# Transposing four units of q and k by DMA instead of TensorE in a fused sparse attention and MLP kernel

## The chip, the core and the metric

The kernel runs on one core of a Trainium2 chip. Five engines run their own instruction streams in order and wait for one another through semaphores: TensorE (PE; its weight loads are shown as PEld), VectorE (DVE), ScalarE (ACT), GpSimd (POOL) and SyncE (SP). SP and POOL issue nearly all DMAs here, each through its own queue; sixteen DMA engines serve both queues. The metric is the device time of one execution in microseconds (us), as the median of several runs.

## The reference

```
q, k, v: (8 batches, 8 heads, 576 tokens, 64), float32
scores = q k^T / 8
heads 0-3 (local):   key j allowed for query i when 0 <= i - j < 32
heads 4-7 (strided): key j allowed when j <= i and j % 32 == i % 32
x = softmax(scores) v, heads side by side: (4608 tokens, 512)
out = relu(x w_in)^2 w_out        w_in: 512 x 2048, w_out: 2048 x 512
```

## The kernel before

Attention of a later batch is woven into the dense work of an earlier one. The dense work runs in nine chunks of 512 tokens. Each chunk has 16 groups of `mm1` (four matmuls of 128x512 each; ACT applies relu, line 713, and DVE squares, line 714) and then 16 groups of `mm2` (four matmuls each; after every fourth, ACT copies the result and SP stores it, lines 733 and 737). `mm1` of chunk 1 writes to two PSUM banks in turn (the pool "ph"). Groups are numbered through: 0 to 15 are `mm1` of chunk 0, 16 to 31 its `mm2`, 32 to 47 `mm1` of chunk 1, 48 to 63 its `mm2`, and so on.

The order of everything else is written out by hand in the string PLAN. A line "35: T8kv" says that step T of unit 8, name k, with its copy on DVE ("v"; "a" is ACT), is put into the instruction streams just before group 35. No scheduler changes this order, so an instruction that waits holds everything behind it on its engine.

A unit u is a batch and a pair of heads: batch u // 4, pair u % 4. Units 8 and 9 are the local heads of batch 2, units 12 and 13 those of batch 3. The local scores (step S, line 505) need q and k with the 64 channels of two heads on the partitions and the tokens in order along the free axis. For batches up to 3 this takes these steps:

- `l` (lines 281 to 292): POOL issues a DMA that loads q or k of both units, float32 to bf16, into a part of `xt` that is not in use yet. Each of 96 partitions gets six neighbouring tokens, so rows are long.
- `c` (cast_qk_local, line 297): a copy on DVE or ACT rearranges one unit into a tile of `qk_in`.
- `T` (step_T, lines 448 to 461): six TensorE transposes (line 453) into a PSUM bank, then one copy (line 460) from PSUM that also brings the tokens into order: on the partition axis they came as "p", in the six blocks as "j", and the copy writes "(p j)".

The results lie in `qT` (a ring of four buffers) and `kTl` (four buffers, chosen by `v_slot`). Local heads of batches 4 to 7 load rows in another shape (step Q, line 278) and are transposed by DMA straight into place (step Y, transpose_local, line 378).

The strided heads of a batch take: C (line 349), a POOL load of q or k rows into `q_t` or `k_t`, one buffer each; X (line 354), a transposing DMA on SP into `qT_s` or `kT_s`; k (lines 365, 368), copies of k into block-diagonal form `kb`; s (line 574), scores, an exponential on ACT and a mask on DVE; x (lines 585 and 588), sums and outputs, a logarithm and an exponential on ACT (590, 591) and products on DVE (598, 604) into `xt`. Since `q_t` and `k_t` have one buffer each, C of the next batch waits on POOL until X of this one has landed. A step "s2.0" is part 0 for batch 2.

Other steps named below: D (line 667) is the product of local weights and v; E brings its result into `xt`, from batch 2 on by a transposing DMA on SP (line 682 in the profile); V and U load v; B copies v into block-diagonal form (line 397).

SP's queue holds, in program order, the transposing DMAs (X, Y, E) and the output stores.

Of the kernel before, what the change touches and what calls it, by code (L numbers as in the profile page):

```python
# [9 lines left out]
BF16 = mybir.dt.bfloat16  # L10
# [18 lines left out]
6: o2 l2k8+9 mv0g o3 mk0g  # L29
10: c4qv  # L30
11: c4kv
12: l2q8+9 T4qa
13: c5qv c5ka T4kv
14: W1q0v T5qa
15: S4!
16: W1q1v T5ka
# [5 lines left out]
22: B11v l3k12+13 s1.2 U2  # L42
23: E4a D5.1
24: x1.0
26: X2k l3q12+13 x1.1
28: V3 E5a x1.2
29: c9kv
30: c8qv
31: c8ka c9qv X2q
34: C3q  # L50
35: T8kv
37: T9kv
38: T8qv C3k
41: S8!
42: T9qa
44: S9! D8.0 k20v
45: D8.1 k21v
46: B20v
47: E8 D9.0 B21v U3
48: Q16k s2.0  # L60
49: D9.1
50: Q17q Q16q c12kv s2.1
51: c12qa E9 s2.2
52: Q17k c13kv c13qa
54: x2.0
55: X3q X3k
56: x2.1 C4k C4q
57: T12ka
58: V4 T13qv T12qa
59: T13ka  # L70
60: x2.2 B30v
61: B31v
63: U4 S12!
# [83 lines left out]
def kernel(  # L157
# [9 lines left out]
    nc = tc.nc  # L167
    B, H, S, D = q.shape
    d_model, d_ff = moe_w_in.shape
    T = B * S  # L170
# [3 lines left out]
    QL = 96  # L174
# [15 lines left out]
    qkT = ctx.enter_context(tc.tile_pool(name="qkT", bufs=4))  # L190
# [17 lines left out]
    def bank(nm):  # L208
        if places:
            return all_banks[places.pop(0)]  # L210
        t = banks[nm].pop(0)
        banks[nm].append(t)
        while id(t) in unread:
            run_due(lambda x: x[1] == unread[id(t)])
        return t
# [10 lines left out]
    NV = 4  # L226
# [12 lines left out]
    kTl = [singles.tile([128, 32 + S], BF16, name=f"kTl{i}") for i in range(NV)]  # L239
# [18 lines left out]
    units = [(b, p) for b in range(B) for p in range(H // 2)]  # L258
    st = {}
# [34 lines left out]
    def cast_qk_local(u, name, copy):  # L294
        s = st[u]
        t = qk_in.tile([QL, 6, 2, D], BF16, name=f"{name}_l")
        copy(t.rearrange("p j h d -> p h j d"), s[name + "f"].rearrange("p h (j d) -> p h j d", j=6))
        s[name] = t
# [16 lines left out]
    def step_TS(b, name, g, copy):  # L315
        src = str_rows[b, name]
        pt = bank("pt").bitcast(BF16)[:, 0:S]
        if b:
            for i in range(NJ):
                c = 128 * (NJ * g + i)  # L320
                nc.tensor.transpose(pt[:, SP_ * i:SP_ * (i + 1)], src[:, c:c + 128], ident[0:SP_, 0:SP_])
            if g == 0:
                o = strTs[name].tile([128, NP2 * SR], BF16, name=f"{name}T_s")
                str_T[b, name] = o.rearrange("c (a p) -> c a p", p=SR)
            copy(str_T[b, name][:, NJ * g:NJ * (g + 1), 0:SP_], pt.rearrange("c (a p) -> c a p", p=SP_))
            return
        for i in range(2):
            for s3 in range(NP3):
                c = 128 * (2 * g + i)
                o = S // 2 * i + QL * s3  # L330
                nc.tensor.transpose(pt[:, o:o + QL], src[:, s3, c:c + 128], ident[0:QL, 0:QL])
        if g == 0:
            o = strTs[name].tile([128, 2 * NJ * SR], BF16, name=f"{name}T_s")
            str_T[b, name] = o[:, 0:2 * NJ * SP_].rearrange("c (a r) -> c a r", a=NJ // 2)
        o = str_T[b, name]
        copy(o[:, 2 * g:2 * g + 2, :].rearrange("c a r -> c (a r)"), pt)
        if g == 1:
            for i in range(2):
                st.setdefault(2 + i, {})[name + "T"] = \
                    o[:, :, 2 * SP_ * i:2 * SP_ * (i + 1)].rearrange("c a (h p) -> c h a p", h=2)  # L340
# [11 lines left out]
    def transpose_str(b, name):  # L352
        o = strTs[name].tile([128, NP2 * SR], BF16, name=f"{name}T_s").rearrange("c (a p) -> c a p", p=SR)
        nc.sync.dma_start_transpose(out=o, in_=big.pop((b, name)))
        str_T[b, name] = o
# [14 lines left out]
    def transpose_local(u):  # L370
        s = st[u]
        for name in "qk":
            if name == "k":
                full = kTl[v_slot(u)]
                dst = full[:, 32:32 + S]
            else:
                full = dst = qkT.tile([128, S], BF16, name="qT")
            nc.sync.dma_start_transpose(out=dst.rearrange("c (t p) -> c t p", p=QL),
                                        in_=s[name].rearrange("p t h d -> p (t h d)"))
            s[name + "T"] = full  # L380

    def v_slot(u):
        b, p = units[u]
        return (b * 2 + p % 2) % NV
# [23 lines left out]
    def shift_v_local(b, copy):  # L408
        t = vl_all[:, (2 * b) % NV:(2 * b) % NV + 2].rearrange("p u h t d -> p (u h) t d")
        copy(t[0:32, :, 1:NL, 0:D], t[96:128, :, 0:NL - 1, 0:D])  # L410
# [37 lines left out]
    def step_T(u, name, copy):  # L448
        s = st[u]
        src = s[name].rearrange("p j h d -> p (j h d)")  # L450
        pt = bank("pt").bitcast(BF16)[:, 0:S]
        for j in range(6):
            nc.tensor.transpose(pt[:, QL * j:QL * (j + 1)], src[:, 128 * j:128 * (j + 1)],  # L453
                                ident[0:QL, 0:QL])
        if name == "k":
            full = kTl[v_slot(u)]
            dst = full[:, 32:32 + S]
        else:
            full = dst = qkT.tile([128, S], BF16, name="qT")
        copy(dst.rearrange("c (p j) -> c p j", j=6), pt.rearrange("c (j p) -> c p j", j=6))  # L460
        s[name + "T"] = full
# [278 lines left out]
    A, V, G = nc.scalar.copy, nc.vector.tensor_copy, nc.gpsimd.tensor_copy  # L740
    ENG = {"a": A, "v": V, "g": G}
# [18 lines left out]
    def warm(n):  # L760
        if n:
            pw = bank("py")
            for _ in range(n):
                nc.tensor.matmul(pw, idle[:, 0:128], idle, start=True, stop=True)
# [3 lines left out]
    def first_part(kks, ffs):  # L768
        for ff in ffs:
            mm1(0, ff, kks, FIRST, None if ff < 2 else "py")  # L770

    def run_step(word):
        word, _, at = word.partition("/")
        places[:] = [int(x) for x in at.split(",") if x]
        op, arg = word[0], word[1:]
        if op == "w":
            warm(int(arg))
        elif op == "c":
            cast_qk_local(int(arg[:-2]), arg[-2], ENG[arg[-1]])
        elif op == "T":  # L780
            step_T(int(arg[:-2]), arg[-2], ENG[arg[-1]])
        elif op == "W":
            step_TS(int(arg[0]), arg[1], int(arg[2]), ENG[arg[3]])
        elif op == "S":
            u, _, half = arg.rstrip("!").partition(".")
            step_S(int(u), int("!" in arg), [int(half)] if half else range(2))
        elif op == "G":
            step_G(int(arg))
        elif op == "b":
            step_B(*(int(x) for x in arg.split(".")))  # L790
        elif op == "N":
            step_N(int(arg))
        elif op == "O":
            step_O(int(arg))
        elif op in "sx":
            (step_SS if op == "s" else step_XX)(*(int(x) for x in arg.split(".")))
        elif op == "k":
            step_K(int(arg[0]), int(arg[1]), ENG[arg[2]])
        elif op == "m":
            memset_later(arg[:-1], nc.gpsimd if arg[-1] == "g" else nc.vector)  # L800
        elif op == "D":
            if "." in arg:
                u, part = arg.split(".")
                step_D(int(u), int(part))
            else:
                step_D0(int(arg))
        elif op == "E":
            step_E(int(arg.rstrip("av")), ENG.get(arg[-1]))
        elif op == "P":
            first_part(*([int(x) for x in y] for y in arg.split(".")))  # L810
        elif op == "H":
            shift_v_local(int(arg[:-1]), ENG[arg[-1]])
        elif op == "C":
            load_str_tall(int(arg[:-1]), arg[-1])
        elif op == "Q":
            load_qk_rows(int(arg[:-1]), arg[-1])
        elif op == "X":
            transpose_str(int(arg[:-1]), arg[-1])
        elif op == "Y":
            transpose_local(int(arg))  # L820
        elif op == "V":
            load_v_local_all(int(arg))
        elif op == "U":
            load_v_str(int(arg))
        elif op == "B":
            spread_v_str(int(arg[0]), int(arg[1]), ENG[arg[2]])
        elif op == "l":
            load_qk_local_sw(int(arg[0]), [int(x) for x in arg[2:].split("+")], arg[1])
        elif op == "r":
            load_str_rows(int(arg[0]), arg[1])  # L830
        elif op == "i":
            load_w_in(int(arg))
        elif op == "o":
            load_w_out(int(arg))
        elif op == "z":
            late_constants()
        else:
            raise ValueError(word)
# [143 lines left out]
```

## Time and profile before

| what | value |
|---|---|
| time, median of 3 runs | 299.3 us (299.23 to 299.55) |
| the profiled execution: its time, its span | 300.02 us, 298.3 us |
| granted TensorE clock in it | 1.0 |
| PE busy, share of the span | 289.5 us, 97% |
| DVE, ACT, POOL busy | 176.6, 172.2, 74.1 us |
| lines 707 and 729 on PE (the two dense products) | 132.1 and 125.3 us busy |
| line 453 (TensorE transposes of q and k) | 96 matmuls, of which 48 in the eight steps of batches 2 and 3 |
| copies of line 460, mean | DVE 752 ns, ACT 639 to 657 ns |
| casts of line 297, bf16 | DVE 347 to 409 ns, ACT 825 ns |
| line 354 (X) and 378 (Y), issue to landing, median | 6.3 and 4.6 us |

Busy time alone does not say what sets the end: an instruction can be issued in time and still hold its engine in a wait. So the sections that follow also use the chain of work that ended last, which goes back from the last instruction to what released each one, and the timelines of single engines.

### The profile page before, as it was taken

To read this page: it belongs to the slowest core of one execution; us is meant where nothing else is said; L and a number is where in the kernel's file an instruction comes from. 1 tells how busy PE (TensorE), PEld (TensorE's weight loads), DVE (VectorE), ACT (ScalarE), POOL (GpSimd) and SP (SyncE) were. 2 spreads that over 40 slices of the span, in tenths; PEclk is the share of its full clock that TensorE was granted. 3 is DMA by queue.
4 is the path that set the end of the run, shared out by engine and by line. 5 is a ranking of instruction groups with operands and counts; after the bars stand their busy time and mean duration, and the time that the engine had idled before them with its cause. 6 is when DMAs were issued, how large, how long until landed. Compare 5 with 4: busy or idle time off the path is not lost.

```text
span 298.3 us, 5654 instructions
## 1 busy us (share of the span) xinstructions
PE 289.5 (97%) x2136; PEld 146.0 (49%) x2172; DVE 176.6 (59%) x457; ACT 172.2 (58%) x324; POOL 74.1 (25%) x107
## 2 busy tenths in 40 slices
PE   7989999999999999999999999999999999999996
PEld 2644555544544544444455445544454444444445
DVE  6657689668768694598267945685484534104400
ACT  3758846696667735773477547645665257126511
POOL 8973743005404008138303800000000000000000
PEclk9999999999999999999999999999999999999999
DMA  7999999999999999999997998621011110010012
GB/s 146 188 208 205 193 199 185 145 196 160 133 155 191 152 155 175 146 155 175 199 194 120 171 190 120 108 57 70 35 23 54 66 43 0 35 74 35 0 70 73
DMA packets 93131, 37.28 MB, mean 125 GB/s; under 512 B 78956, under 2 KB 87238, under 8 KB 93104
## 3 DMA queue, kind: packets, MB, share of 16 engines
q0 software_dynamic: 54448, 18.82, 59.1%
q1 hardware_dynamic: 38512, 18.03, 31.7%
q8 instruction: 17, 0.28, 0.4%
q14 instruction: 10, 0.08, 0.1%
q10 hardware_dynamic: 144, 0.07, 0.1%
HBM read 38.21 MB, written 9.44 MB: 160 GB/s over the span
## 4 chain that ended last, share of the span: by engine, by line
PE 89%; DMA 6%; issue 2%; ACT 1%; DVE 1%; SPq 0%; POOL 0%; DVEq 0%; ACTq 0%; POOLq 0%
PE psb L729 40%; PE psb L707 37%; DMA qT_s<-q_t 4%; DMA w_out_b<-in_k_dram 2%; PE psb L667 2%; PE psb L574 1%; PE psb L588 1%; PE psb L754 1%; PE psb L585 1%; PE psb L453 1%; PE psb L505 1%; PE psb L550 1%; ACT r L713 1%; DVE xt L635 0%; PE psb L475 0%
## 5 line engine op out<-in xcount | busy, mean ns | idle before, releaser
L707 PE MATMUL psb<-xt,w_in_b 128*128 128x512 bf16 x558 | 132.1, 379 | 1.2 <-DVE xt L635 0.2
L729 PE MATMUL psb<-w_out_b,g_sb 128*128 128x512 bf16 x542 | 125.3, 379 | 1.3 <-issue 0.6
L713 ACT ACTIVATE r<-psb 128x512 bf16<-128x512 f32 x144 | 85.5, 600 | 37.5 <-PE psb L707 34.0
L714 DVE TENSOR_TENSOR g_sb<-r 128x512 bf16<-128x512 bf16 x144 | 60.8, 424 | 73.6 <-ACT r L713 72.8
L707 PEld LDWEIGHTS <-w_in_b 128*128 128x128 bf16 x576 | 53.4, 98 | 58.8 <-issue 1.3
L729 PEld LDWEIGHTS <-g_sb 128*128 128x128 bf16 x560 | 51.8, 98 | 57.3 <-DVE g_sb L714 0.3
L733 ACT COPY y<-psb 128x512 f32<-128x512 f32 x35 | 20.6, 590 | 53.2 <-PE psb L729 50.2
L598 DVE TENSOR_TENSOR xt<-psb,rv 64x144 bf16<-64x144 f32 x84 | 34.1, 406 | 9.0 <-ACT rv L591 7.9
L590 ACT ACTIVATE rv<-psb 128x432 f32<-128x432 f32 (+1 forms) x21 | 10.5, 500 | 9.8 <-PE psb L585 9.8
L673 DVE TENSOR_TENSOR x_l<-psb,rinv 96x384 bf16<-96x384 f32 x28 | 15.5, 553 | 1.0
L349 POOL DMA_DIRECT2D q_t<-in_q_dram x6 | 3.2, 542 | 46.1 <-DMA qT_s<-q_t 28.2
L604 DVE TENSOR_TENSOR xt<-psb,rv 64x270 bf16<-64x270 f32 (+1 forms) x28 | 11.0, 433 | 3.7 <-ACT rv L591 3.5
L278 POOL DMA_DIRECT2D k_l<-in_k_dram x16 | 11.9, 754 | 4.2 <-ACT kTl L460 2.8
L575 ACT ACTIVATE e<-psb 128x432 bf16<-128x432 f32 (+1 forms) x21 | 10.4, 496 | 4.2 <-PE psb L574 4.0
L418 POOL DMA_DIRECT2D vl<-in_v_dram x7 | 10.1, 1442 | 6.3 <-PE psb L550 2.1
L278 POOL DMA_DIRECT2D q_l<-in_q_dram x16 | 11.6, 736 | 0.0
L561 ACT ACTIVATE e<-psb 128x384 bf16<-128x384 f32 x24 | 9.6, 509 | 3.4 <-PE psb L550 3.4
L591 ACT ACTIVATE rv<-rv 128x432 f32<-128x432 f32 (+1 forms) x21 | 11.2, 533 | 0.7
L557 DVE TENSOR_TENSOR e<-e,mask_all 128x576 bf16<-128x576 bf16 x16 | 6.7, 458 | 7.5 <-ACT e L561 7.5
L667 PEld LDWEIGHTS <-e 128*128 128x128 bf16 x168 | 8.6, 101 | 4.6
L349 POOL DMA_DIRECT2D k_t<-in_k_dram x6 | 3.4, 561 | 29.1 <-DMA kT_s<-k_t 27.2
L667 PE MATMUL psb<-vl,e 128*128 128x65 bf16 x168 | 9.5, 195 | 0.1
(117 smaller groups left out, 215.8 us busy)
## 6 DMA issues: line engine op xcount, KB each, us to landing
out_dram<-y SPq DMA_DIRECT2D x35, 256.0 KB, 3.4
vl<-in_v_dram POOLq DMA_DIRECT2D x7, 384.0 KB, 8.4
w_out_b<-in_moe_w_out_dram POOLq DMA_DIRECT2D x4, 512.0 KB, 15.5
q_t<-in_q_dram POOLq DMA_DIRECT2D x7, 288.0 KB, 5.9
k_t<-in_k_dram POOLq DMA_DIRECT2D x7, 288.0 KB, 6.5
v_st<-in_v_dram POOLq DMA_DIRECT2D x7, 216.0 KB, 8.5
w_in_b<-in_moe_w_in_dram POOLq DMA_DIRECT2D x2, 704.0 KB, 13.9
k_l<-in_k_dram POOLq DMA_DIRECT2D x16, 72.0 KB, 7.1
```

The lines of the kernel that those rows point to most:

```text
L278: nc.gpsimd.dma_start(out=t[:, :, hh, :], in_=src[b, 2 * p + hh].rearrange("(t p) d -> p t d", p=QL))
L590: nc.scalar.activation(rv, pn, AF.Ln)
L591: nc.scalar.activation(rv, rv, AF.Exp, scale=-1.0)
L598: nc.vector.tensor_tensor(to[:, :, NJ * part:NJ * (part + 1), par], of, by, op=ALU.mult)
L604: nc.vector.tensor_tensor(t, of[:, g:, :, lo:lo + k], by[:, g:, :, lo:lo + k], op=ALU.mult)
L667: nc.tensor.matmul(po[0:m, n, :], e[:, c:c + m], rhs[:, NL * part + n, 0:D + 1], start=True, stop=True)
L673: nc.vector.tensor_tensor(x, po[0:QL, :, 0:D], rinv[0:QL].to_broadcast([QL, NL, D]), op=ALU.mult)
L707: nc.tensor.matmul(ph, w_in_b[:, kk, 128 * ff:128 * (ff + 1)], xt[kk][:, 512 * c:512 * (c + 1)], start=(kk == order[0]), stop=(kk == order ...
L713: nc.scalar.activation(r, ph, AF.Relu)
L714: later(1, lambda: nc.vector.tensor_tensor(g[:, ff, :], r, r, op=ALU.mult))
L729: nc.tensor.matmul(py, g[:, ff, 128 * j:128 * (j + 1)], w_out_b[:, ff, :], start=(ff == 0), stop=(ff == 15))
L733: nc.scalar.copy(y, py)
```

## The change

Units 8, 9, 12 and 13 no longer use step T. After the cast, step A (transpose_cast) issues a transposing DMA on SP's queue, from the cast tile into a buffer in SBUF, still in six blocks. Step R (order_local) then copies that buffer into place on DVE or ACT, bringing the tokens into order; it reads SBUF where the copy of step T read PSUM. For k, step A writes into the `kTl` buffer two places further on, and `k_slot` gives batches 3 to 7 the other pair of `kTl` buffers than `v_slot` did. For q, step A takes one more buffer of the `qT` ring.

In PLAN the casts move forward: those of batch 2 from groups 29 to 31 to groups 25 to 29, those of batch 3 from groups 50 to 52 to groups 39 to 43. Step X2k moves from group 26 to group 29. One cast of batch 2 goes from ACT to DVE, and the copies change engines in part. Two lines of batch 1 are regrouped with the same steps in almost the same order (c5q moves ahead of T4k by one group).

```diff
-12: l2q8+9 T4qa
-13: c5qv c5ka T4kv
+12: l2q8+9 T4qa c5qv
+13: c5ka T4kv
...
-26: X2k l3q12+13 x1.1
-28: V3 E5a x1.2
-29: c9kv
-30: c8qv
-31: c8ka c9qv X2q
+25: c8kv A8k
+26: l3q12+13 x1.1 c9kv A9k
+28: V3 E5a x1.2 c8qv A8q
+29: c9qv A9q X2k
+31: X2q
 34: C3q
-35: T8kv
-37: T9kv
-38: T8qv C3k
-41: S8!
-42: T9qa
+37: R8kv
+38: C3k R8qa
+39: c12ka A12k
+40: R9kv c13ka A13k
+41: S8! R9qa
+42: c12qv A12q
+43: c13qv A13q
 44: S9! D8.0 k20v
...
-50: Q17q Q16q c12kv s2.1
-51: c12qa E9 s2.2
-52: Q17k c13kv c13qa
+50: Q17q Q16q s2.1
+51: E9 s2.2
+52: Q17k
 54: x2.0
-55: X3q X3k
-56: x2.1 C4k C4q
-57: T12ka
-58: V4 T13qv T12qa
-59: T13ka
+55: X3q X3k R12kv
+56: x2.1 C4k C4q R12qa
+57: R13ka
+58: V4 R13qv
...
+    def transpose_cast(u, name):
+
+        t = kTl[(k_slot(u) + 2) % NV][:, 32:32 + S] if name == "k" else qkT.tile([128, S], BF16, name="qT")
+        nc.sync.dma_start_transpose(out=t.rearrange("c (j p) -> c j p", p=QL),
+                                    in_=st[u][name].rearrange("p j h d -> p (j h d)"))
+        st[u][name + "6"] = t
+
+    def order_local(u, name, copy):
+        s = st[u]
+        if name == "k":
+            full = kTl[k_slot(u)]
+            dst = full[:, 32:32 + S]
+        else:
+            full = dst = qkT.tile([128, S], BF16, name="qT")
+        copy(dst.rearrange("c (p j) -> c p j", j=6), s[name + "6"].rearrange("c (j p) -> c p j", j=6))
+        s[name + "T"] = full
+
+    def k_slot(u):
+
+        return (v_slot(u) + 2 * (units[u][0] > 2)) % NV
```

More of the change, by code (lines that the diff above doesn't have):

```diff
@@ L373, in transpose_local @@
             if name == "k":
-                full = kTl[v_slot(u)]
+                full = kTl[k_slot(u)]
                 dst = full[:, 32:32 + S]
@@ L380, in transpose_local @@
             s[name + "T"] = full
+    def transpose_cast(u, name):
[6 more added lines that the diff above has]
+        if name == "k":
+            full = kTl[k_slot(u)]
+            dst = full[:, 32:32 + S]
[5 more added lines that the diff above has]
+        return (v_slot(u) + 2 * (units[u][0] > 2)) % NV
     def v_slot(u):
@@ L455, in step_T @@
         if name == "k":
-            full = kTl[v_slot(u)]
+            full = kTl[k_slot(u)]
             dst = full[:, 32:32 + S]
@@ L818, in run_step @@
             transpose_str(int(arg[:-1]), arg[-1])
+        elif op == "A":
+            transpose_cast(int(arg[:-1]), arg[-1])
+        elif op == "R":
+            order_local(int(arg[:-2]), arg[-2], ENG[arg[-1]])
         elif op == "Y":
```

## The prediction, before the change was run

> **What bounds the kernel now.** I read the page first (busy shares, DMA, chain), then the chain of waits from 56 us on, then the timelines of SP, ACT and PE there, then DMA packets by queue in short windows.
>
> ```profile
> PE 289.5 (97%) x2136; PEld 146.0 (49%) x2172; DVE 176.6 (59%) x457; ACT 172.2 (58%) x324; POOL 74.1 (25%) x107
> DMA  7999999999999999999997998621011110010012
> ```
>
> TensorE is busy for 97% of the span, so what leaves its stream shortens the kernel, if no wait fills the place. But the DMA engines are above nine tenths in nearly every slice up to two thirds of the span: until then the DMA engines are as full as PE.
>
> ```profile
> 56.38 0.58 SPq L737
> 56.96 0.04 issue
> 57.00 11.70 DMA qT_s<-q_t
> 68.70 0.04 issue
> 68.74 0.36 PE psb L574 x8
> ...
> 76.94 0.18 PE psb L585
> 77.12 0.21 PE psb L588 x8
> 77.34 0.86 PE psb L729 x4
> 78.20 0.26 PE psb L453 x6
> ```
>
> In the chain of waits (start us, us, what) one DMA stands before the strided scores of batch 2 (step s2.0, line 574): the transposed load of q (step X2q), issued at 57.00 behind three output stores (L737) on SP's queue and landed at 68.70. PE starts 0.04 us after. The last line prices a TensorE transpose step (L453): its six matmuls advance the chain by 0.26 us.
>
> ```profile
> 52.15 3.07 SPq L354 DMA_TRANSPOSE kT_s<-k_t  x1
> 55.27 1.69 SPq L737 DMA_DIRECT2D out_dram<-y  x3
> 57.00 5.09 SPq L354 DMA_TRANSPOSE qT_s<-q_t  x1
> 62.14 0.58 SPq L737 DMA_DIRECT2D out_dram<-y  x1
> 67.53 1.21 SPq L682 DMA_TRANSPOSE xt<-x_l  x1
> ```
>
> SP's timeline: X2k at 52.15, when its rows have landed, then stores, then X2q. SP issues nothing from the start-up loads until X2k.
>
> ```profile
> 68.74 0.36 PE L574 MATMUL psb<-qT_s,kb 128*128 128x54 bf16 x8 [0.36 <-DMA qT_s<-q_t]
> ```
>
> On PE the wait cost 0.36 us: X2q has no slack at all, and each microsecond that it lands later is one on PE.
>
> ```profile
> 60.51 0.60 ACT L713 ACTIVATE r<-psb 128x512 bf16<-128x512 f32 x1 [0.27 <-PE psb L707]
> 61.00 1.31 ACT L521 ACTIVATE e<-psb 128x288 bf16<-128x288 f32 x4
> 62.16 0.64 ACT L713 ACTIVATE r<-psb 128x512 bf16<-128x512 f32 x1
> 62.64 0.69 ACT L460 COPY qT<-psb 128x576 bf16<-128x576 bf16 x1
> 63.16 1.35 ACT L713 ACTIVATE r<-psb 128x512 bf16<-128x512 f32 x2
> ```
>
> ACT in the first matrix product: each group's relu (L713) must empty one of two banks ("ph") before the next group but one. A relu starts 0.2 us after its group and takes 0.60, and a group takes 0.86: the slack is 0.06 us. Back to back, starts are 0.49 us apart after a relu, 1.16 after the four exponentials, 0.52 after a copy.
>
> ```profile
> q1 hardware_dynamic: 842, 0.22, 90.9%
> q0 software_dynamic: 754, 0.20, 68.5%
> ```
>
> DMA packets from 57 to 61 us: SP's queue (q1) and POOL's (q0) go about packet for packet, and both have a backlog.
>
> **The change, part by part.** *Taken from PE:* eight step_T, four before s2.0 (T8k, T9k, T8q, T9q), four after (batch 3): 8 x 0.26 = 2.08 us, all on the path. Eight PSUM places go too, which no wait shows as scarce.
>
> *Casts.* Batch 2's four casts (L297) move from groups 29 to 31 up to 25 to 29, all on DVE, which runs line 598 and 604 without a gap from 45.04 to 51.70. Their k rows landed at 44.4 (issued 30.55, 13.9 us), q at 48.7: no wait. Two casts, 0.35 each, now stand ahead of the last line 604, which moves to 52.4; group 32's fourth matmul needs it at 51.76 + 3 x 0.216 = 52.4. I charge 0.1 (0 to 0.3). Batch 3's casts move from 50 to 52 up to 39 to 43; those of k are on ACT, 0.82 each, 0.72 apart. k's rows landed at 57.3 (issued 42.24, 15.1 us).
>
> *Copies.* Eight copies remain (0.75 on DVE, 0.64 on ACT from PSUM; read from SBUF bounded by 0.35, the cast's rate, and 0.83, ACT's cast). I keep the old prices; on DVE nobody waits. What counts is ACT's place: in groups 38 to 42 it had one (T9q); now it has R8q, c12k, c13k and R9q, ahead of relus. Played through with the spacings above and PE groups of 0.86, counted from 51.76: relu 37 ends 57.75; R8q 57.64 to 58.28; relu 38 ends 58.76, group 40 waits 0.16. c12k, 58.65 to 59.48; relu 39 ends 59.97; S8's scores run 59.70 to 60.07, and c13k to 60.69; relu 40 ends 61.18, group 42 waits 0.32. Exponentials to 62.23, R9q to 62.75, relu 41 ends 63.35, and group 43, due at 62.11, starts at 63.42: 1.31. Together 1.8 us of new waiting, which eats the 1.04 of the four steps: PE, which stood ready for s2.0 at 68.74 - 0.36 = 68.38, would reach it at 68.38 - 1.04 + 1.8 + 0.1 = 69.2. If R8q waits for A8q, or c12k for its rows, this grows one for one.
>
> *DMAs on SP.* Eight transposes of 147 KB are new. Nearest row: line 378's, of the same shape: 1.21 us to issue, landing 2.5 us on where nothing else runs, up to 6.0 beside POOL's loads; x_l's, also of that shape, up to 8.4. Three in a row (issued 99.46, 100.78, 102.80) landed at 104.2, 104.8, 105.4: 0.6 apart. Program order is now A8k, A9k, A8q, a store, A9q, X2k (moved from group 26 to 29, past these), two stores, X2q, a store, then A12k, A13k, A12q, A13q, and only then E8, E9, X3q, X3k. A8k can go at 48.0, A9k at 50.8, A8q at 52.8; A9q and X2k follow at 54.4 and 55.9.
> X2q's landing: both queues are full until 70.5, so four transposes ahead push it by their own time, 4 x 0.6 = 2.4: 71.1. Lower bound, the A's all vanish in SP's idle queue before 55: the one store that now precedes X2k lands before it, 0.8 off, 67.9. Upper: X2k, issued at 55.9, takes its 10.9 and X2q follows it by 4.8 (5.6 before, less that store), 71.6, plus 2 if POOL's delayed loads, larger packets, now run beside X2q. I take 71.1, nearest to the measured full queue.
> [...]
>
> *POOL* waits with C3q for X2q (18.2 us before) and so moves with it, as do C3k, U3 and the Q16 and Q17 loads. X3k landed at 89.5, its copies into kb ended at 91.6 and s3.0 came at 93.10: 1.5 of slack. X3k moves by 2.4 with POOL, and by up to 4 x 0.6 more for batch 3's transposes; PE's own shift there is 2.4 - 1.04 = 1.4. The wait at s3.0 is between 0 (the first alone) and 4.8 - 2.9 = 1.9; I charge 0.5, near the low end, since q1 moved only 24 packets between 71 and 74 us and has room. E8 and E9 come some 5 us later; their tokens are first read at group 64 (86 us): cover enough. R12 and R13 at groups 55 to 58 (75 to 80 us) meet landings near 72 to 78; ACT has room there.
>
> *Buffers.* k_slot gives batches from 3 on the other kTl pair; A8k writes what S5 read by 37 us. The qT ring of four now turns twice as fast: A13q needs R9q, 63 us, and is issued after 70. Nothing.
>
> **Sum.** s2.0 at 71.15 instead of 68.74: +2.4 (it covers PE's 69.2). Batch 3: -1.04. s3.0: +0.5. Together +1.9. The profiled execution took 300.02 (span 298.3 and 1.7 around it), 0.7 above the median of 299.3; it becomes 301.9, the median 301.2.
>
> **Rivals.**
> *Hidden (faster).* The A's run in SP's idle queue and X2q lands at 69.2 or sooner. For it: SP issues nothing before 52. Against: POOL's queue is full then. s2.0 comes at 69.2 at the earliest by ACT's count, or 68.7 if that is too strict; -1.04 after it: 298.3 to 298.7. Deciding point: X2q by 69.2.
> *ACT's wait decides (slower).* c12k or R8q blocks ACT: POOL's load of k, delayed from 57.3 by the A's, or A8q, issued at 52.8 with a latency like E9's 8.4 (61.2). Above 2 us of such waiting PE reaches s2.0 after 71.15; at 3.5, 72.7: sum +3.5, 302.8. For it: both are within 2 us of their readers; against: 5 to 6 us is usual.
> *X3k decides (slower).* Batch 3's transposes stand between C3's loads of 4 KB packets, like E9, and X3 slides by 2 more: s3.0 waits 1.9 or more: 303 to 304.
> *One 128x128 block at a time.* If a DMA transpose moved its blocks singly at the shortest landing seen, 2.5 us for 4.5 blocks, 4 x 2.5 us instead of 2.4 would lie ahead of X2q: 7.6 more, 308.8. Against: landings 0.6 apart. [...]
>
> **How the numbers follow.** About 0.2% (0.6 us) is what a measurement of this kernel can tell from no change. Forecast: 0.60, its own range 299.7 to 303; of it 0.06 falls within 0.2%. Hidden: 0.20, of which 0.05 within. ACT: 0.10. X3k: 0.08. Blocks: 0.02. Slower 0.54 + 0.10 + 0.08 + 0.02 = 0.74, same 0.11, faster 0.15. The range for eight in ten reaches from the hidden case, 298.3, to X3k's, 304.
>
> **What would show it.** Right: qT_s landing after 70, with the wait before line 574 at 1 to 3 us; PE waits of about 1.3 us near 62 on relu 41; no line 453 on PE after 34 us; the copies of qT from SBUF on ACT at 58 and 62. Wrong: X2q landing by 69 and line 574 without a wait; or ACT idle on A8q for several us near 58; or a wait before 93 on kb longer than 2 us.

## The result, and the profile after

The changed kernel takes **309.07 us** (307.41 to 309.59, median of six), the kernel before on the same chip 299.67 us (299.23 to 300.11). The ratio is **1.030, with a 95% interval of 1.027 to 1.033**: 9.4 us slower, where the prediction said 1.9 slower and ended its range at 304.0. The profiled execution has a span of 307.4 us against 298.3. Here and below a ratio leaves out executions over 1.5% longer than the fastest of their kernel (in e8 one of 510.76 us), so it need not be that of the medians.

The page of the changed kernel, busy time and the granted clock in 40 slices of 7.7 us:

```profile
PE 291.8 (95%) x2124; PEld 144.6 (47%) x2124; DVE 176.7 (57%) x458; ACT 173.4 (56%) x323; POOL 74.2 (24%) x107
...
PE   7899999729999999999999999999999999999996
...
PEclk9999999969999999999999999999999999999999
```

The whole loss is one hole in PE's row, in the eighth and ninth slices (54 to 69 us), and in the ninth slice the granted clock falls too. The answer on waits (who waited for whom: us in total, times, longest) names it:

```profile
PE psb L729 <- ACT r L735: 8.5, 2, 7.8
...
ACT qT L397 <- DMA qT<-q_l: 7.2, 1, 7.2
...
DVE kTl L397 <- DMA kTl<-k_l: 3.7, 1, 3.7
...
PE psb L729 <- DVE xt L626: 0.4, 1, 0.4
```

(Lines have moved: 729 is the first dense product, 707 before; 735 its relu, 713 before; 386 is step A, 397 the copy of step R, 298 the cast, 596 the strided scores of s2.0, 574 before.) ACT stands for 7.2 us in R8q, the first copy of q, because its transpose A8q has not landed. The relus are behind it on ACT, PE gets no free bank, and waits for 7.8 us. The chain (start us, us, what) shows the same in order:

```profile
52.89 0.36 PE psb L729
53.26 12.14 DMA qT<-q_l
...
65.42 0.02 ACT qT L397
...
66.48 0.60 ACT r L735
...
67.12 1.88 PE psb L729 x4
...
77.95 0.20 PE psb L596 x8
```

A8q is issued at 53.26 and lands 12.14 us later. Step s2.0, which came at 68.74 before, comes at 77.95, 9.2 us late; the span grew by 9.1, so the loss is complete there. s3.0 is 8.2 us late (101.3 instead of 93.1); the 1.0 gained between the two is lost again further on, most of it at 151 us, where PE waits 0.7 us for a later batch's transposing DMA into `kTl` (line 572). X2q, the transfer that held s2.0 before, is now issued at 67.13 and lands at 73.39, and PE does not wait for it.

SP's timeline (start, duration of the issue, what; a row of x2 reaches from the start of the first issue to the end of the second):

```profile
47.98 4.55 SPq L386 DMA_TRANSPOSE kTl<-k_l  x2
53.26 4.37 SPq L386 DMA_TRANSPOSE qT<-q_l  x1
...
58.30 2.10 SPq L386 DMA_TRANSPOSE qT<-q_l  x1
60.49 5.44 SPq L355 DMA_TRANSPOSE kT_s<-k_t  x1
```

The four A's are issued at 47.98, 51.32, 53.26 and 58.30 and land at 61.54, 63.99, 65.40 and 67.69: 13.6, 12.7, 12.1 and 9.4 us after issue and some 2 us apart. Batch 3's four, issued from 70.34 on, land 3.2 to 7.1 us after issue, the first two 0.65 apart, the other two, with POOL's next loads beside them, 3.4 and 3.2 behind the one before. What differs is in the packets by queue (packets, MB, share of 16 engines), first from 57 to 61 us, then from 71 to 75:

```profile
q0 software_dynamic: 627, 0.29, 105.8%
q1 hardware_dynamic: 343, 0.08, 61.5%
...
q1 hardware_dynamic: 2804, 1.00, 112.5%
```

From 57 to 61 us POOL's queue (q0) still works on loads, and SP's (q1) moves 86 packets per us; from 71 to 75, alone, it moves 701. A transposed unit is 576 packets of 256 bytes: 6.7 us at the first rate, 0.8 at the second. Before, in the window that the prediction quoted, q1 made 842 in 4 us, 211 per us.

### The profile page after: what moved, and what is told of

It is laid out like the page before. It is cut to its first block, busy times and chain, and to the rows that moved or that the text cites. A ratio compares the mean times of both kernels' runs of the same rounds, so it can differ in the third digit from the quotient of the medians.

```text
span 307.4 us, 5613 instructions
## 1 busy us (share of the span) xinstructions
PE 291.8 (95%) x2124; PEld 144.6 (47%) x2124; DVE 176.7 (57%) x458; ACT 173.4 (56%) x323; POOL 74.2 (24%) x107
## 4 chain that ended last, share of the span: by engine, by line
PE 82%; DMA 9%; DVE 4%; issue 2%; ACT 2%; SPq 1%; POOL 0%; DVEq 0%; ACTq 0%; POOLq 0%
PE psb L729 37%; PE psb L751 35%; DMA qT<-q_l 4%; DMA kTl<-k_l 3%; DMA w_out_b<-in_k_dram 2%; PE psb L689 2%; DVE xt L620 1%; PE psb L596 1%; PE psb L776 1%; PE psb L527 1%; PE psb L610 1%; PE psb L607 1%; ACT r L735 1%; PE psb L572 1%; PE psb L475 1%
## 5 line engine op out<-in xcount | busy, mean ns | idle before, releaser
L729 PE MATMUL psb<-xt,w_in_b 128*128 128x512 bf16 x576 | 134.5, 381 | 9.2 <-ACT r L735 8.5
L751 PE MATMUL psb<-w_out_b,g_sb 128*128 128x512 bf16 x560 | 127.6, 379 | 0.0
L626 DVE TENSOR_TENSOR xt<-psb,rv 64x270 bf16<-64x270 f32 (+1 forms) x28 | 10.9, 433 | 2.5 <-ACT rv L613 2.2
```

The lines of the kernel that those rows point to most:

```text
L626: nc.vector.tensor_tensor(t, of[:, g:, :, lo:lo + k], by[:, g:, :, lo:lo + k], op=ALU.mult)
L729: nc.tensor.matmul(ph, w_in_b[:, kk, 128 * ff:128 * (ff + 1)], xt[kk][:, 512 * c:512 * (c + 1)], start=(kk == order[0]), stop=(kk == order ...
L751: nc.tensor.matmul(py, g[:, ff, 128 * j:128 * (j + 1)], w_out_b[:, ff, :], start=(ff == 0), stop=(ff == 15))
```

## The experiments

All ratios are against the kernel before, run on the same chip beside them.

### Batch 2 or batch 3?

e1_batch2 does batch 2 by DMA and batch 3 by TensorE as before; e2_batch3 the other way round. The core of each edit, against the changed kernel:

```diff
-39: c12ka A12k
-40: R9kv c13ka A13k
+40: R9kv
...
+57: T12ka
+58: V4 T13qv T12qa
+59: T13ka
```

```diff
-25: c8kv A8k
-26: l3q12+13 x1.1 c9kv A9k
-28: V3 E5a x1.2 c8qv A8q
-29: c9qv A9q X2k
...
+26: X2k l3q12+13 x1.1
...
+35: T8kv
+37: T9kv
...
```

> Batch 2's four transposes by DMA, batch 3 as before (TensorE transposes, late casts). Theory 'landing': the transposes of batch 2 land 12 us after their issue, the copy of q on ACT waits for one of them and PE stands still behind ACT; all of the loss is made in batch 2, so the step s2.0 is again 9 us late and the time is 299.7 + 9.2 = 309 us (308 to 310.5), with a wait of 7 to 8 us on PE near 59 us. Rival 'crowding': a good part of the loss is from batch 3's transposes in the DMA queues; then 303 to 306 us.

> Batch 3's four transposes by DMA, batch 2 as before. Theory 'landing': here 12 to 15 groups lie between a transpose and its copy, nobody waits, four TensorE steps of 0.26 us go: 299.7 - 1.0 = 298.7 us (298.2 to 299.7, the upper end if the two casts on ACT hold PE for up to 1 us). Rival 'crowding': X3 and E8, E9 come later and s3.0 waits: 301 to 303 us.

e1: 310.62 us, ratio 1.036 (1.030 to 1.041). e2: 301.54 us, ratio 1.0047 (1.0017 to 1.0077). The waits of e1:

```profile
PE psb L727 <- ACT r L733: 8.3, 1, 8.3
ACT qT L395 <- DMA qT<-q_l: 7.7, 1, 7.7
```

Batch 2's half is the whole loss, by the same wait, as expected but for 0.1 us of the range. Batch 3's half, from which the prediction took 1.04 us, gains nothing that shows by itself; its expectation was missed by 2.8 us. The median lies in the range of its rival, crowding, but the wait before s3.0 that the rival named is not on PE's list.

### Is it the reading or the traffic?

e3_unread issues the four A's of batch 2 as the changed kernel does, but nobody reads what they bring: batch 2 goes through step T as well. e4_late_read keeps batch 2 by DMA and moves the copies R and all that reads them 7 to 12 groups later; batch 3 goes by step T in both.

```diff
-37: R8kv
-38: C3k R8qa
...
-41: S8! R9qa
...
+35: T8kv
+37: T9kv
+38: T8qv C3k
+41: S8!
+42: T9qa
```

```diff
-37: R8kv
-38: C3k R8qa
...
+38: C3k
...
+46: B20v R8kv
+47: B21v U3 R8qa
+48: Q16k s2.0 R9kv
+49: R9qa
+50: Q17q Q16q c12kv s2.1 S8!
...
+53: S9!
```

> As the run with batch 2 alone, but the four transposed tiles are read by nobody: units 8 and 9 use the TensorE transposes at their old places, so the DMAs are pure load. This gives the price of the traffic without the wait for it. Theory 'landing': X2q still lands near 73 us behind the four, s2.0 starts there instead of at 68.7: 299.7 + 4.5 = 304 us (302.5 to 305); the rest of the 9 us is the wait. If the time is 309 us the wait on ACT is not the cause; if it is under 300.5, the traffic costs nothing.

> As the run with batch 2 alone, but the copies R8, R9 and what reads them (S8, S9, D8, D9, E8, E9) come 7 to 12 groups later, R8 at 46, R8q at 47. The four transposes are issued as before. Theory 'landing': no copy waits, PE does not stand near 59 us, and what is left is X2q at 73 us, as in the run with unread tiles: 303 us (302 to 305), 6 us less than with the early reads. If it stays at 307 to 309 the place of the reads is not the cause.

e3: 308.53 us, 1.028 (1.022 to 1.034). e4: 316.15 us, 1.052 (1.046 to 1.058). Both miss their expectation by far, and to the same side. The chain of e3:

```profile
60.88 11.20 DMA kT_s<-k_t
...
72.17 0.38 DVE kb L365
72.54 0.15 DVE kb L368
72.70 0.38 DVE e L548
...
73.12 0.53 PE psb L688 x6
```

Nobody reads an A here, and still PE stands for 5.5 us: X2k, behind the A's on SP's queue, lands at 72.08 (62.53 in e7, further on), DVE waits for it in the copy into kb (line 365), and the mask that the local outputs need (line 548) is behind that copy. In e4 the wait is one further on, at X2q itself, and a second one follows at the transpose of E9:

```profile
PE psb L592 <- DMA qT_s<-q_t: 7.4, 1, 7.4
PE psb L725 <- DMA xt<-x_l: 4.6, 1, 4.6
```

So the loss is not ACT's wait. That is merely the first of several readers, each of which costs PE a wait of 5 to 8 us (7.8, 5.5 and 7.4 here); e3's expectation had said that 309 us would mean this. The traffic itself is late, and all that stands in SP's queue with it.

### Are the transposes slow, or is it what runs beside them?

e5_fewer_loads is the changed kernel without POOL's loads of batch 3's local q, k and v (960 KB); e6_fewer_loads_before is the kernel before without the same loads. Batch 3's local heads are not computed in either.

```diff
+        if b == 3:
+            for i, u in enumerate(us):
+                st.setdefault(u, {})[names + "f"] = st[8 + i][names + "f"]
+            return
...
-        nc.gpsimd.dma_start(out=t[:, :, :, :, 0:D].rearrange("p u h t d -> p (u h t) d"), in_=src)
+        if b != 3:
+            nc.gpsimd.dma_start(out=t[:, :, :, :, 0:D].rearrange("p u h t d -> p (u h t) d"), in_=src)
```

> The changed kernel without POOL's loads of batch 3's local q, k and v (960 KB issued between 42 and 50 us): units 12 and 13 take batch 2's rows and batch 1's v instead, so batch 3's local heads are not computed. Theory 'packets': SP's queue gets about one 256-byte packet for each packet of POOL's queue, and beside loads with packets of 768 to 4096 bytes that is some 100 packets a us, 5 to 6 us for a transpose of 576 packets. With these loads gone A8q lands near 59 instead of 65.4 us, PE's wait behind ACT falls from 7.8 to 1 to 3 us, X2q lands near 67: 300 to 303 us. Rival 'slow transposes': a transpose is slow by itself, 3 to 4 us each, one after the other; then A8q still lands after 62 and the time is 306 to 309 us.

> The kernel before without the same loads (batch 3's local heads not computed), to compare the last run with. Both theories: X2q, which lands at 68.7 us beside these loads, lands at 64 to 66 us, the wait of 0.36 us before s2.0 goes: 298.8 to 299.5 us.

e5: 302.72 us, 1.011 (1.008 to 1.014). e6: 299.93 us, 1.002 (1.000 to 1.004). The change costs 2.8 us without these loads and 9.4 with them. e5 is where it was expected; e6 misses by 0.4 us, though X2q lands at 61.52 and its wait is gone. The four A's of e5, issued at 51.61, 54.56, 56.51 and 58.38, land 5.6, 3.1, 2.5 and 2.6 us later, and SP's issues of them are short (1.2 to 1.3 us each, not up to 4.4). Its packets by queue, from 57 to 61 us:

```profile
q1 hardware_dynamic: 1479, 0.58, 60.5%
```

No packet of q0 is left in this window, q1 moves 370 per us, and a part of the 4 us it has nothing to do.

These short landings are in part an accident. The profiled e5 (304.04 us, the longest of its four) had a granted clock of 0.51 from 12.0 to 22.4 us and reached s1.0 at 42.1 us, 3.5 later than e6, so its A's were issued late, when fewer loads were under way. e9, further on, lacks the same loads without that accident: its A's, issued at 47.60, 50.51, 52.46 and 54.33, take 10.7 to 6.2 us, and land at 58.3 to 60.6, with e5's at 57.2 to 61.0. So what the missing loads bring forward is the landing (A8q at 59.0 and 59.4, not 65.4), and not every transfer is short. The accident does not make the ratio: the other three executions of e5 took 301.97 to 303.12 us. The wait that remains in e5:

```profile
PE psb L734 <- ACT r L740: 2.2, 2, 1.7
```

### Does the place in SP's queue decide?

e7_unread_behind puts the four unread A's of e3 behind X2q, and X2k back to its old place. e8_unread_two issues only two of them, those of k, at the place of the changed kernel. Against the changed kernel (the steps R become T as in e3):

```diff
-25: c8kv A8k
-26: l3q12+13 x1.1 c9kv A9k
-28: V3 E5a x1.2 c8qv A8q
-29: c9qv A9q X2k
-31: X2q
+25: c8kv
+26: X2k l3q12+13 x1.1 c9kv
+28: V3 E5a x1.2 c8qv
+29: c9qv
+31: X2q A8k A9k A8q A9q
```

```diff
-28: V3 E5a x1.2 c8qv A8q
-29: c9qv A9q X2k
+28: V3 E5a x1.2 c8qv
+29: c9qv X2k
```

> As the run with four unread transposes (308.5 us), but X2k is back at group 26 and the four are issued behind X2q at group 31. Same number of DMAs, other place in SP's queue. Theory 'packets': X2k and X2q land at 63 and 68.7 us as in the kernel before, s2.0 is in time; the four now delay E8, E9 and X3 a little, as batch 3's did in the run with batch 3 alone (301.5 us): 300 to 303 us. If the time stays above 306, the transposes hurt wherever they stand in the queue.

> As the run with four unread transposes (308.5 us), but only the two of k are issued (A8k, A9k at groups 25 and 26). Theory 'packets': half the packets ahead of X2k, which lands near 67 instead of 72 us, X2q near 70; the copies into kb hold DVE for 1 to 2 us: 302 to 304.5 us, about half of the loss. Rival: if the loss comes from the issue of q's two transposes (which held SP for 4 us each), it vanishes: under 300.5 us.

e7: 301.61 us, 1.011 (1.004 to 1.017), with a profiled span of 299.7. e8: 307.92 us, 1.026 (1.022 to 1.030). SP's timeline of e7, and then of e8:

```profile
51.94 2.93 SPq L354 DMA_TRANSPOSE kT_s<-k_t  x1
...
56.51 5.24 SPq L354 DMA_TRANSPOSE qT_s<-q_t  x1
61.86 4.27 SPq L385 DMA_TRANSPOSE kTl<-k_l  x2
```

```profile
48.76 4.14 SPq L385 DMA_TRANSPOSE kTl<-k_l  x2
...
53.63 7.01 SPq L354 DMA_TRANSPOSE kT_s<-k_t  x1
...
61.85 4.05 SPq L354 DMA_TRANSPOSE qT_s<-q_t  x1
```

With the same bytes behind X2q, X2k and X2q land at 62.53 and 68.33 (63.09 and 68.70 before), and most of the loss is gone, as expected. With half of the bytes ahead, the loss is not half, as was expected, but nearly all of it: X2k holds SP for 7.01 us, X2q is issued at 61.85 and lands at 72.61, and PE waits 3.3 us for it; behind that wait the granted clock was 0.50 from 72.4 to 75.8 us, and four matmuls of the dense product took 1.89 us there, against 1.03 ahead of the wait. What stands ahead of X2k and X2q in the queue decides here; the number of transposes ahead counted less than linearly (1.028 with four in e3, 1.026 with two in e8). e7 does not tell the place from the time: its four are issued from 61.86 on, when all but one of POOL's loads have landed.

### ScalarE's share, and two attempts to mend it

e9_fewer_loads_dve is e5 with the copies R8q, R9q and the casts c12k, c13k on DVE. e10_loads_late computes everything, with POOL's loads of batch 3's local rows moved behind the A's, batch 3 by TensorE, R8q and R9q on DVE, and batch 3's score steps some groups later. e11_batch3_later is e2 with all four casts on DVE and the readers of X3k later. Their edits, against e5, the changed kernel and e2:

```diff
-38: C3k R8qa
-39: c12ka A12k
-40: R9kv c13ka A13k
-41: S8! R9qa
+38: C3k R8qv
+39: c12kv A12k
+40: R9kv c13kv A13k
+41: S8! R9qv
```

```diff
-22: B11v l3k12+13 s1.2 U2
-26: l3q12+13 x1.1 c9kv A9k
-28: V3 E5a x1.2 c8qv A8q
...
+38: C3k l3k12+13 l3q12+13 V3 R8qv
...
+58: V4 T12ka
+59: T12qa
+60: x2.2 B30v T13qv
+61: B31v T13ka
...
+74: s3.0
```

```diff
-39: c12ka A12k
-40: c13ka A13k
+40: c12kv A12k
...
+42: T9qa c13kv A13k
...
-66: Y17 k30v
...
+69: k30v
...
+74: s3.0
```

> The run without batch 3's loads on POOL's queue (302.7 us), with the copies R8q and R9q and the casts c12k and c13k on VectorE instead of ScalarE; batch 3's local heads are not computed here, as there. Theory "ScalarE's copies are the rest": the 2.8 us that this pair of kernels still differs by is ScalarE's queue, where two copies of 1.17 us and casts stand ahead of the relus that TensorE reads (2.2 us of TensorE waiting for them); on VectorE a copy took 0.64 us, so the wait falls to 0.3 us or less and the time to 298.5 to 300.5. Rival "the rest is elsewhere" (the tail, the clock, VectorE as the new wait): 302 or more, with TensorE's wait moved to VectorE's rows.

> Everything computed. Batch 2 goes by DMA transposes as in the changed kernel, but POOL's loads of batch 3's local k, q and v are issued at group 38, behind the transposes, instead of groups 22 to 28; batch 3's local rows, which then come too late for a DMA transpose, are transposed by TensorE at groups 58 to 61, and the four copies of batch 2 are VectorE's. The score steps of batch 3 follow up to 4 groups later. Theory "packets": the four transposes land 3 to 6 us after issue as in the run without these loads, X2q lands before its reader, TensorE waits at most 1 us around group 38; 298.5 to 301. Rival "transposes are slow by themselves": they land 10 us or more after issue again and the time is 305 or more.

> Everything computed. Batch 3 alone by DMA transposes, with its four casts on VectorE at groups 40 to 44, and the steps that read the late transpose X3k (k30, k31, s3, x3) 2 to 4 groups later. Against the run of batch 3 alone (301.5 us): theory "X3k's landing is what batch 3's half costs": the wait in front of s3.0 goes and ScalarE is rid of two casts; 298.5 to 299.5. Rival "transposes crowd the loads of the middle": the loss of 1.4 to 2 us stays, 300.5 to 302.

**e9:** 301.86 us, 1.0055 (1.0024 to 1.0086); e5 was at 1.011 (1.008 to 1.014). The wait behind ACT is gone from PE's list, as expected, and about half of what was left with it. In the profiled execution s2.0 comes at 68.3, as in e6 (68.2): without these loads and with the copies on DVE, batch 2's half no longer delays s2.0, though its 1.04 us are not gained there either. The time missed the 298.5 to 300.5, for another wait has come, as the rival had it (its 302 us or more was missed by 0.1), at X3k's copy into kb (X3k landed at 92.27, in e6 at 88.18):

```profile
PE psb L601 <- DVE kb L370: 2.9, 2, 2.6
```

**e10:** median 311.5 us (306.15 to 316.07), ratio 1.022 (1.018 to 1.027); the profiled execution is the one of 316.07, so that the sizes below are those of its longest. X2k and X2q came in time (63.23 and 66.78), and nothing waited for an A. But the A's landed 11.1, 8.9, 7.4 and 6.3 us after issue, not 3 to 6: they were issued 3 us earlier than in e5 and landed no sooner, at 59.4 to 61.8, for POOL's older loads were still under way until 59.71. And the loads that were moved back met the next X's. Neither expectation holds as it was put. The wait and the chain from 84 us:

```profile
PE psb L691 <- DVE e L551: 8.2, 1, 8.2
```

```profile
72.97 24.31 DMA v_st<-in_v_dram
```

A load of v took 24.31 us, DVE stood in its copy, and the masks of batch 3 behind that copy cost PE 8.2 us: the same kind of hole, 30 us later. How much of it the two shortest executions have (306.15 and 307.38) is not shown.

**e11:** 301.42 us, 1.0036 (1.0008 to 1.0064), against 1.0047 for e2. The median is in the range of its rival again. In its profiled execution PE waits for nothing from 60 to 130 us, s3.0 among it, and the time has hardly moved: X3k's landing is not what batch 3's half costs. The gain is there at first: s4.2 comes at 127.2 us, 1.4 earlier than before (0.4 of it already at s2.0). It is lost in a wait for a later batch's transposing DMA into `kTl`, which landed at 142.12 (138.67 before), and at s5.0 PE is 0.3 behind the kernel before:

```profile
PE psb L576 <- DMA kTl<-k_l: 1.5, 1, 1.5
```

That this DMA lands later because of the change is not shown. The times range from 299.46 to 305.08 us in e2 and from 299.23 to 306.22 in e11, and what the longer ones lose is open.

No kernel here beats the one before.

## Why the prediction was wrong

**Direction and place held.** Slower was given 0.74. It named SP's queue between 48 and 73 us, X2q pushed by the four A's, R8q as a copy that could block ACT, and the relus behind it. A8k, A9k and A8q were issued at 47.98, 51.32 and 53.26, for which it had 48.0, 50.8 and 52.8. Eight steps T have left PE's list. DVE's casts cost 0.4 us, a little above their bounds of 0 to 0.3.

**The step that failed** is the price of a transposing DMA in this stretch, which stands in the prediction twice: "four transposes ahead push it by their own time, 4 x 0.6 = 2.4", for X2q, and "5 to 6 us is usual", against a late A8q. The second decided the time: A8q took 12.14 us and landed at 65.40, for a copy that the prediction had at 57.64. In the first, X2q landed 4.7 us later than before, not 2.4. The 0.6 came from three landings with q1 to itself (batch 3's first two are again 0.65 apart). Beside POOL's loads the four landed 2.05 us apart ((67.69 - 61.54) / 3), after 9.4 to 13.6 us, and not the 2.5 to 8.4 that the nearest rows gave. The line that speaks against the 0.6 was quoted in the prediction, and read only for its ratio of packets: 842 of q1 in 4 us, with both queues busy, is 211 per us, and 576 packets are then 2.7 us, four of them 10.9: more than the 2.05 apiece and the 4.7 of X2q that came of it, but no 0.6. Nearer still is X2k of the kernel before, a transposing DMA issued in this very stretch, at 52.15: it took 10.95 us to land, and A8q, issued at 53.26, took 12.14. The prediction used this 10.95 for X2k's upper bound, and 8.4 at most for the A's ahead of it. In the trace no one rate holds for a transpose: four units of 147 KB in 19.7 us, from A8k's issue to A9q's landing, are 30 GB/s beside loads, and a unit in 0.65 us is 226 GB/s with the queue alone.

**SP's order** failed with it. A9q and X2k were put at 54.4 and 55.9 and came at 58.30 and 60.49, since the issue of A8q held SP for 4.37 us and that of A9q for 2.10, where the nearest row had 1.21; X2k's then held it for 5.44. X2q landed at 73.39 (71.1 forecast). It did not decide, for an earlier reader of SP's transfers, R8q, had already stopped ACT.

**The rival "ACT's wait decides"** is what happened, with 0.10 and 302.8 us. Its condition (A8q after 61.2) and its rule (one for one) were right, its size was not: by that rule a R8q at 65.42 instead of 57.64 puts s2.0 at 69.2 + 7.8 = 77.0, and 77.95 was measured. On PE's row the 9.2 us at s2.0 are: 8.5 of waiting for the relu (7.8 and 0.65), 0.4 for DVE, 1.4 at the lower clock (below), less 1.04 for the four steps T and 0.36 for the wait that was at s2.0 before, 8.9 in all; 0.3 is left unassigned. e3 and e4 show that a repair of this wait alone would have met the next.

**Hidden (0.20)** needed X2q by 69.2: the A's did go into SP's idle time, and ran against POOL's loads. **X3k decides:** in the changed kernel PE does not wait between 78 and 102 us, since PE came 8 us late itself; in e9, where PE came earlier, X3k's copies cost 2.6 us. **One block at a time** gave 308.8, near the result by luck: its rate of 2.5 us each is excluded by the landings, 0.65 apart with the queue alone and 2.05 beside loads.

**ACT's own order**, charged with 1.8 us, is seen by itself in e5: 2.2 us. The terms were off, though: a copy R on ACT took 1.17 us, nearly twice the 0.64 that the prediction kept.

**Batch 3's -1.04** is not seen in any time: e2 and e11 are at or above the kernel before, though PE has four steps T less there. The traces of the changed kernel and of e11 show it made by s3.0 or s4.2 and lost later, in waits of 0.7 and 1.5 us for a transposing DMA into `kTl`, for which the prediction had no term.

What stays open: whether q1's low rate beside q0 comes from how the two queues share the DMA engines or from the transposes themselves. The runs show only that it follows POOL's loads. In the changed kernel, e5, e9 and e10, POOL's last load issued ahead of A8k landed at 63.77, 56.75, 58.49 and 59.71, and the four A's at 61.5 to 67.7, 57.2 to 61.0, 58.3 to 60.6 and 59.4 to 61.8, though A8k was issued at 47.98, 51.61, 47.60 and 48.27.

## What to carry to other kernels

Price a transfer by a like one in the same stretch of the trace, or by its queue's packets per us in a window in which the same queues are busy together, not by its landings when it is alone: here that says 11 us to landing and 2.7 apiece, where 12.1 and 2.05 were measured, and the landings alone said 2.5 and 0.6. Before a DMA is put ahead of another on a queue in order, look at what the queue's next transfers have as slack, and at which copy on a compute engine would wait for it with that engine's other work behind it. Idle issue slots of SP were no sign of free DMA engines here: in the changed kernel SP issued nothing from 1.7 to 47.98 us, while the core moved 200 GB/s from 40 to 48 us.

## What the runs showed of the hardware that was not expected

**Both queues got slower together.** From 53 to 59 us the core moved 115 GB/s in the changed kernel and 145 before. From 57 to 61 us, with transposes beside loads, q0 and q1 together made 243 packets per us and 93 GB/s in the changed kernel; from 71 to 75 us q1 alone made 701 and 249. POOL's loads paid too: the load of k for batch 3 landed at 59.64 (57.3 before) and the last of q at 63.77 (61.5 before). In packets the shares of q1 and q0 from 57 to 61 us are nearly equal before (842 against 754) and not after (343 against 627); why, no run here shows.

**The granted clock fell to 0.50 in a long wait of PE.** Windows of the changed kernel (start and end, us; PE, PEld, DVE, ACT, POOL busy; granted clock, DMA share, GB/s), then PE's timeline:

```profile
59.00:63.00 4.00, 0.31 (x2) 0.03 (x1) 0.98 (x2) 0.00 (x0) 0.00 (x0) 1.00 1.44 116
63.00:66.00 3.00, 0.00 (x0) 0.00 (x0) 0.00 (x0) 0.58 (x1) 0.00 (x0) 0.58 1.65 191
66.00:69.00 3.00, 1.88 (x8) 0.49 (x9) 1.11 (x3) 3.00 (x5) 0.00 (x0) 0.50 1.47 153
...
73.00:78.00 5.00, 5.00 (x58) 2.61 (x56) 4.81 (x16) 3.50 (x9) 1.07 (x2) 1.00 1.11 172
```

```profile
67.12 1.87 PE L729 MATMUL psb<-xt,w_in_b 128*128 128x512 bf16 x4 [7.81 <-ACT r L735]
...
72.43 1.02 PE L729 MATMUL psb<-xt,w_in_b 128*128 128x512 bf16 x4 [0.65 <-ACT r L735]
```

After 7.81 us of waiting the first four matmuls took 1.87 us instead of 1.02, at a clock of 0.50, and the clock was back at 1.00 from 71 us. In the wait, which began at 59.31, it was 1.00 until 63 us and 0.50 from 64 on. In e9 it fell with a shorter wait, of 2.59 us (1.00 until 93.8 us, 0.51 from 94.3 to 97.3), and in e5 it was at 0.51 from 12.0 to 22.4 us, with PE busy and no wait over 0.96 us since 5 us. So a long wait is not all that a low clock came with; what sets it, no run here shows. The hole in PE's stream cost 0.85 us here beyond its length, 0.24 more in the scores behind them and 0.37 in the next eight matmuls (2.26 us, against 1.89 for eight from 75 us on).

**A reordering copy from SBUF was slow on ACT and not on DVE.** Groups of the changed kernel (busy us, mean ns): step R from SBUF, step T from PSUM, on ACT and on DVE:

```profile
L397 ACT COPY qT<-qT 128x576 bf16<-128x576 bf16 x3 | 3.5, 1170 | 7.2 <-DMA qT<-q_l 7.2
...
L482 ACT COPY qT<-psb 128x576 bf16<-128x576 bf16 x3 | 1.9, 634 | 1.2 <-PE psb L475 1.2
...
L482 DVE COPY qT<-psb 128x576 bf16<-128x576 bf16 x1 | 0.8, 758 | 0.2 <-PE psb L475 0.2
L397 DVE COPY qT<-qT 128x576 bf16<-128x576 bf16 x1 | 0.7, 652 | 0.0
```

The same elements in the same order took ACT 1,170 ns from SBUF and 634 from PSUM; on DVE SBUF was the faster, 652 against 758. The prediction had bounded both by 0.35 and 0.83 us.
